# First attention batch: q and k loaded in rows of four tokens, queries turned and keys summed by TensorE

## The chip, the cores and the metric

One core of one Trainium2 chip runs the whole kernel. The metric is the device time of one execution in microseconds; before the change it is 1469.86 us, the median of three runs (1468.98 to 1470.56).

## What is computed

Attention over pooled keys and values, then two feed-forward blocks, all in float32:

```python
# q, k, v: (8 batches, 8 heads, 576 tokens, 64)
k_p = k.reshape(B, H, Sp, 8, D).mean(axis=3)      # keys and values are means over eight tokens
v_p = v.reshape(B, H, Sp, 8, D).mean(axis=3)
scores = scale * np.matmul(q, k_p.transpose(0, 1, 3, 2))
attn = softmax(scores)                            # 576 x 72 for each head
x = np.matmul(attn, v_p)                          # to (4608 tokens, 512)
x = ((x @ w1) * (x @ w2)) @ w3 @ w_out            # d_ff 1024
h = x @ w_in                                      # d_ff 2048
out = (h / (1 + np.exp(-1.702 * h))) @ w_out2
```

The weights are float64. They are loaded as pairs of 32-bit words and turned into float32 on the chip.

## The kernel before

The kernel has three stages. In the first, 40 weight tiles are loaded (`Conv.load`, L151, 512 KB each), converted (`Conv.step`: two passes of ScalarE, L166 and L168, a shift on VectorE, L169, an integer sum on GpSimd, L172) and split into a rounded part and a rest (`split`, L104 and L105). The sixteen tiles of `w3` among them are turned by TensorE (L508) and multiplied with `w_out` (`w3_mm`, by `mm3`, L114 to L116, into the banks `acc0` and `acc1`), so that the two matrices become one. `mm3` makes one product of near-float32 precision from three products of rounded parts, 128 x 512 each. In the second stage nine blocks of 512 tokens go through `w1`, `w2` and the combined matrix; in the third they go through the second feed-forward block (L709 and on). From about 118 us on, TensorE runs the products of the second and third stages almost without a gap.

The attention is cut into 32 groups: one batch and two heads each (`NG`). The steps of a group (`g0` to `g6`) are spread over calls of `tick`: one call for each step of the weight conversion in the first stage, two for each of the eight steps of a block in the second. The first batch's four groups (`NPE`, numbers 0 to 3) run in the first stage by `tick_first`, which overlaps two groups. They use two sets of banks in turn (`banks_of`): `wk[2:]` for even groups, `acc[2:]` for odd ones.

What the change touches is the beginning of a group. `g_load(n)` brings k and q (tiles `kr` and `qr`, 128 partitions x 576) by `load_blocks`: four DMAs for each, whose pieces are 32 numbers of one token (128 B), so that each 32 x 32 block stands where VectorE's block transpose turns it into place. `g0(n)` then makes, on VectorE, `kT` from `kr` (L255), `qT` from `qr` (L256), and the sums of eight tokens `ks` from `kT` (L258). ScalarE copies them to the two corners of `kbd` (L260, L261), so that one product serves both heads, and the load of the next group is issued. `g1(n)` multiplies `qT` with `kbd` on TensorE (L277, five products of 144 columns) into the group's two banks, and VectorE takes the maxima and differences. Later steps take the exponential (L293), normalise it (L300 to L303), turn it (`g4`: TensorE for the first four groups, L351 to L361), and multiply it with the pooled values (`g6`, L380 to L383).

All loads are issued by SP's queue, in one order. A scheduler arranges each engine's instructions when the kernel is built; each engine and each queue then works through its own list in order.

Of the kernel before, what the change touches and what calls it, by code (L numbers as in the profile page):

```python
# [7 lines left out]
F32 = mybir.dt.float32  # L8
# [4 lines left out]
ALU = mybir.AluOpType  # L13
# [4 lines left out]
P = 128  # L18
T = 512
# [3 lines left out]
def pooled_attention_moe_moe2(  # L23
# [18 lines left out]
    nc = tc.nc  # L42
    B, H, S, D = q.shape
    NT, DM = out.shape
    POOL = 8
    SK = S // POOL
# [9 lines left out]
    NPE = HP  # L56
# [28 lines left out]
    def take(shape=(P, 2, T), dtype=F32R):  # L85
        pool, i = free.pop(0)
        t = pool.tile(list(shape), dtype, name=f"s{i}", tag=f"s{i}")
        held[id(t)] = (t, pool, i)
        return t

    def take_a(i, dtype=F32R):

        return slota_p.tile([P, 2, T], dtype, name=f"s{i}", tag=f"s{i}")
# [30 lines left out]
    def sl(i, n=P):  # L124
        return slice(i * n, (i + 1) * n)
# [65 lines left out]
    with pa_ctx:  # L191
        pa = pa_ctx.enter_context(tc.tile_pool(name="pa", bufs=1))
# [6 lines left out]
            out=mask[:, 0], in_=mask[:, 0], compare_op=ALU.is_gt, fill=0.0,  # L199
            base=SK, pattern=[[0, D]], channel_multiplier=-1)  # L200
        nc.gpsimd.affine_select(
            out=mask[:, 1], in_=mask[:, 1], compare_op=ALU.is_ge, fill=0.0,
            base=-SK, pattern=[[0, D]], channel_multiplier=1)
        qT = pa.tile([P, TT * P], F32, name="qT")
        nc.vector.memset(qT[:, S:], 0.0)
        kbd = pa.tile([P, 2, SK], F32, name="kbd")
# [4 lines left out]
        for t in s_ts:  # L211
# [3 lines left out]
        ident = pa.tile([P, P], F32, name="ident")  # L215
        nc.gpsimd.memset(ident, 1.0)
        nc.gpsimd.affine_select(
            out=ident, in_=ident, compare_op=ALU.is_equal, fill=0.0,
            base=0, pattern=[[-1, P]], channel_multiplier=1)
        vm = pa.tile([P, 2, 2 * D], F32R, name="vm")  # L220
        vt = pa.tile([96, 2 * D], F32R, name="vt")
        nc.gpsimd.memset(f32(vt), 0.0)
# [2 lines left out]
        g_q, g_k, g_v, g_s = {}, {}, {}, {}  # L225

        def load_blocks(dst, src, b, hp):
            for c in range(4):
                nc.sync.dma_start(  # L229
                    dst[32 * c:32 * c + 32],  # L230
                    src[b, 2 * hp + c // 2, :, 32 * (c % 2):32 * (c % 2) + 32].rearrange(
                        "(g t) d -> t g d", t=32))

        def g_load(n):
            if n >= NG:
                return
            b, hp = divmod(n, HP)
            g_k[n] = pa.tile([P, S], F32, name="kr", tag="raw", bufs=4).rearrange("p (g d) -> p g d", d=32)
            load_blocks(g_k[n], k, b, hp)
            g_q[n] = pa.tile([P, S], F32, name="qr", tag="raw", bufs=4).rearrange("p (g d) -> p g d", d=32)  # L240
            load_blocks(g_q[n], q, b, hp)
# [9 lines left out]

        def g0(n):
            kr, qr = g_k.pop(n), g_q.pop(n)
            kT = pa.tile([P, S], F32, name="kT", tag="kT")
            nc.vector.transpose(out=kT, in_=kr.rearrange("p g d -> p (g d)"))  # L255
            nc.vector.transpose(out=qT[:, :S], in_=qr.rearrange("p g d -> p (g d)"))  # L256
            ks = pa.tile([P, SK], F32, name="ks", tag="ks")
            nc.vector.tensor_reduce(  # L258
                out=ks, in_=kT.rearrange("p (s u) -> p s u", u=POOL), op=ALU.add, axis=AX.X)
            nc.scalar.copy(kbd[:D, 0], ks[:D])  # L260
            nc.scalar.copy(kbd[D:, 1], ks[D:])  # L261
            g_load(n + 1)

        def banks_of(n):
            return acc[2:] if n < NPE and n % 2 else wk[2:]
# [132 lines left out]
        def x_slot(j, c):  # L398
            if (j, c) not in xs:
                xs[j, c] = take()  # L400
            return xs[j, c]
# [3 lines left out]
        def tick_first():  # L405

            t = tick_n[0]
            tick_n[0] += 1
            for n in range(NPE):
                if t == 2 * n + 6:  # L410
                    g6(n)
            for n in range(NPE):
                s = t - 2 * n
                if s == 0 and n == 0:
                    g0(0)
                elif s == 1:
                    g1(n)
                elif s == 2:
                    g2(n)
                    g0(n + 1)  # L420
                elif s == 3:
                    g3(n)
                elif s == 4:
                    g4(n)
                    g_va(n)
                elif s == 5:
                    g_vb(n)
            if t == 2 * NPE + 4:
                tick_n[0] = 4 * NPE
                give(s_sl)  # L430

        def tick():
            t = tick_n[0]
            if t < 4 * NPE:
                return tick_first()
            tick_n[0] += 1
            n, s = divmod(t, 4)
            if s == 0:
                if NPE <= n - 1 < NG:
                    g4(n - 1)  # L440
            elif s == 1:
                if n < NG:
                    g1(n)
            elif s == 2:
                if NPE <= n - 1 < NG:
                    g6(n - 1)
                if n < NG:
                    g2(n)
                    g_va(n)
                if n + 1 < NG:  # L450
                    g0(n + 1)
            elif n < NG:
                g3(n)
                g_vb(n)
# [92 lines left out]
        for jh in range(2):  # L547
            for i in range(4):
                j = jh * 4 + i
# [12 lines left out]

        conv.load()
        g_load(0)
        v_load(0)
        n3 = 8 + 2 * NIT
# [35 lines left out]
        for blk in range(NB):  # L602
            x = [x_slot(blk, c) for c in range(KM)]
            if blk == NB - 2:

                pa_ctx.close()
                pa = pa_ctx.enter_context(tc.tile_pool(name="pc", bufs=1, reuse_waits="tile"))
# [10 lines left out]
            for f in range(NF1):  # L618
# [6 lines left out]
                if blk == NB - 1:  # L625
                    give(w1_s.pop(f))
                    give(w2_s.pop(f))
                    if 0 <= f - FA < KM:

                        t = take_a(f - FA)  # L630
# [8 lines left out]
                u = u_s[blk, f] = take()  # L639
# [32 lines left out]
    with tc.tile_pool(name="pb", bufs=1, reuse_waits="tile") as pb, \  # L672
# [44 lines left out]
        def moving():  # L717
            i = mv_n[0] % NMV
            mv_n[0] += 1
            return pb.tile([P, 2, 2, T], F32R, name="mv", tag=f"mv{i}")  # L720
# [153 lines left out]
        x = x_first  # L874
# [9 lines left out]
        for k, f in enumerate(FO):  # L884
# [10 lines left out]
            g = moving()[:, :, 0]  # L895
# [20 lines left out]
        for pr in range(1, NPAIR + 1):  # L916
# [17 lines left out]
            for fp in range(NFP):  # L934
# [4 lines left out]
                for name, i in ORDER:  # L939
# [6 lines left out]
                    if name in PART:  # L946
                        s, h = PART[name]
# [13 lines left out]
                    elif name == "M2":  # L961
# [4 lines left out]
                        if i:  # L966
                            gelu(g11, g11)
                            g = mvs["M1", fp] = moving()
# [35 lines left out]
            src = {"M5": 0, "M7": 1, "M3": 2, "M2": 3, "M4": 3, "M6": 4}  # L1004
# [12 lines left out]
            m1, U, V, n = [], [], [], 0  # L1017
# [21 lines left out]
            for name, u in OUT:  # L1039
# [5 lines left out]
                if pr == NPAIR and name == "M3":  # L1045
# [7 lines left out]
                    for m in range(2):  # L1053
# [6 lines left out]
                        rows = out[b1 * T:(b1 + 1) * T]  # L1060
# [73 lines left out]
```

## Time and profile before

| | us |
|---|---|
| median of three runs | 1469.86 |
| the profiled execution's own time | 1471.6 |
| its span (first to last instruction) | 1469.5 |
| TensorE products busy | 1434.8 |
| VectorE, ScalarE, GpSimd busy | 985.2, 695.5, 489.3 |

The span is what the rows are taken from; the execution's own time holds 2.1 us around it. A busy share is an average over stages with different limits: here GpSimd works mainly in the first half, the DMA engines are full at the beginning and idle after it, and TensorE is busy nearly everywhere. The time between TensorE's busy time and the span, 34.7 us, is what all its waits come to.

### The profile page before, as it was taken

What the parts mean: (1) busy time and instruction counts of PE and PEld (TensorE: products, weight loads), DVE (VectorE), ACT (ScalarE), POOL (GpSimd) and SP (SyncE); (2) the same over time, 40 slices, a digit from 0 to 9 for tenths busy, and PEclk for the clock granted to TensorE, in tenths of its full rate; (3) what the DMA queues carried; (4) which work ended last, traced back from release to release, by engine and by line L of the source; (5) the groups of instructions that cost most, each with busy time, mean ns of one, the idle gap of its engine ahead of it and who ended that gap; (6) DMA issues with size and microseconds to landing.
All of it is one profiled execution on the core that took longest, in us unless ns stands there. A gap on an engine that the chain in (4) does not pass through costs nothing.

```text
span 1469.5 us, 19435 instructions
## 1 busy us (share of the span) xinstructions
PE 1434.8 (98%) x6536; PEld 1189.6 (81%) x6536; DVE 985.2 (67%) x1728; ACT 695.5 (47%) x1212; POOL 489.3 (33%) x589
## 2 busy tenths in 40 slices
PE   5979999999999999999999999999999999999998
PEld 4867888888888888888888888788888888888886
DVE  7878998878887887655636346783559354954554
ACT  7875344434333334366635334653455244534442
POOL 8789655554545555357743200000000000000000
PEclk9989999999999999999999999999999999999999
DMA  9993233323232311089869979867676766785665
GB/s 271 245 224 57 60 81 62 78 49 78 49 75 52 71 40 37 29 300 341 329 226 380 350 236 311 289 213 230 201 236 225 226 199 222 240 240 181 199 212 140
DMA packets 294435, 267.64 MB, mean 182 GB/s; under 512 B 201664, under 2 KB 226240, under 8 KB 294336
## 3 DMA queue, kind: packets, MB, share of 16 engines
q1 hardware_dynamic: 291648, 265.09, 60.0%
q10 hardware_dynamic: 2688, 1.31, 0.3%
q8 instruction: 52, 0.85, 0.2%
q14 instruction: 47, 0.39, 0.1%
HBM read 209.72 MB, written 56.62 MB: 181 GB/s over the span
## 4 chain that ended last, share of the span: by engine, by line
PE 89%; DMA 3%; DVE 2%; ACT 1%; SPq 1%; POOL 1%; issue 1%; DVEq 0%; ACTq 0%; POOLq 0%
PE bk L709 42%; PE wk L114 9%; PE wk L115 9%; PE wk L116 9%; PE acc L115 4%; PE acc L116 4%; PE acc L114 4%; PE wk L277 2%; DMA s<-in_moe_w_dram 1%; PE bk L116 1%; PE bk L114 1%; PE bk L115 1%; DMA wud<-wt 1%; SPq L229 1%; PE wk L381 1%
## 5 line engine op out<-in xcount | busy, mean ns | idle before, releaser
L709 PE MATMUL bk<-mv,st 128*128 128x512 f32 x1140 | 269.4, 389 | 0.0
L709 PE MATMUL bk<-xM,st 128*128 128x512 f32 x1104 | 262.1, 389 | 0.2 <-ACT u L972 0.2
L709 PEld LDWEIGHTS bk<-mv,st 128*128 128x128 f32 x1140 | 214.0, 188 | 44.4
L709 PEld LDWEIGHTS bk<-xM,st 128*128 128x128 f32 x1104 | 207.1, 188 | 44.0 <-ACT u L972 1.1
L114 PE MATMUL wk<-s,s 128*128 128x512 f32 x576 | 226.9, 396 | 1.9 <-ACT a L638 1.1
L116 PE MATMUL wk<-s,s 128*128 128x512 f32 x576 | 224.9, 391 | 1.3 <-DVE s L105 1.3
L115 PE MATMUL wk<-s,s 128*128 128x512 f32 x576 | 225.2, 392 | 1.0 <-DVE s L391 1.0
L314 DVE STREAM_TRANSPOSE p<-s_t 32x160 f32<-32x160 f32 (+1 forms) x560 | 178.5, 319 | 10.3
L114 PE MATMUL acc<-s,s 128*128 128x512 f32 x352 | 134.3, 404 | 9.3 <-DVE s L105 6.4
L115 PE MATMUL acc<-s,s 128*128 128x512 f32 x352 | 140.7, 400 | 1.2 <-POOL s L105 1.1
L116 PE MATMUL acc<-s,s 128*128 128x512 f32 x352 | 140.3, 398 | 0.0
L114 PEld LDWEIGHTS wk<-s,s 128*128 128x128 f32 x576 | 108.5, 189 | 24.6 <-ACT a L638 1.5
L116 PEld LDWEIGHTS wk<-s,s 128*128 128x128 f32 x576 | 108.5, 188 | 24.1 <-DVE s L105 1.5
L115 PEld LDWEIGHTS wk<-s,s 128*128 128x128 f32 x576 | 108.6, 189 | 23.4 <-DVE s L391 1.8
L105 DVE TENSOR_TENSOR mv<-g,mv 128x1024 fp32r<-128x1024 f32 x80 | 97.8, 1222 | 32.3 <-ACT mv L104 30.4
L104 ACT CAST mv<-g 128x1024 fp32r<-128x1024 f32 x80 | 84.3, 1054 | 72.0 <-PE bk L709 71.6
L172 POOL TENSOR_TENSOR cv<-cv,s 128x512 int32<-128x512 int32 x72 | 97.8, 1368 | 29.5 <-DVE cv L169 19.2
L105 POOL TENSOR_TENSOR s<-a,s 128x512 fp32r<-128x512 f32 x56 | 73.0, 1303 | 82.6 <-ACT s L104 62.7
L638 ACT COPY a<-wk 128x512 f32<-128x512 f32 x72 | 42.1, 585 | 112.1 <-PE wk L116 91.4
L114 PEld LDWEIGHTS acc<-s,s 128*128 128x128 f32 x352 | 67.8, 193 | 24.8 <-ACT s L104 5.0
L369 POOL TENSOR_TENSOR ph<-p,ph 128x576 fp32r<-128x576 f32 x32 | 45.6, 1424 | 125.3 <-ACT ph L368 122.7
L115 PEld LDWEIGHTS acc<-s,s 128*128 128x128 f32 x352 | 67.8, 192 | 15.2 <-POOL s L105 2.3
(190 smaller groups left out, 2355.7 us busy)
## 6 DMA issues: line engine op xcount, KB each, us to landing
st<-wud SPq DMA_DIRECT2D x95, 512.0 KB, 4.2
st<-wind SPq DMA_DIRECT2D x70, 512.0 KB, 4.7
st<-wind SPq DMA_DIRECT2D x70, 256.0 KB, 3.8
s<-in_moe_w_dram SPq DMA_DIRECT2D x32, 512.0 KB, 6.5
wind<-s SPq DMA_DIRECT2D x32, 512.0 KB, 5.5
s<-in_moe_w_out_dram SPq DMA_DIRECT2D x24, 512.0 KB, 6.7
kr<-in_k_dram SPq DMA_DIRECT2D x128, 72.0 KB, 2.6
qr<-in_q_dram SPq DMA_DIRECT2D x128, 72.0 KB, 2.6
```

The lines of the kernel that those rows point to most:

```text
L104: nc.scalar.copy(dst[:, 0], src)
L105: lo_eng.tensor_tensor(out=dst[:, 1], in0=src, in1=f32(dst[:, 0]), op=ALU.subtract)
L114: nc.tensor.matmul(o, a[:, 0, a_sl], b[:, 0, b_sl], start=first, stop=False)
L115: nc.tensor.matmul(o, a[:, 0, a_sl], b[:, 1, b_sl], start=False, stop=False)
L116: nc.tensor.matmul(o, a[:, 1, a_sl], b[:, 0, b_sl], start=False, stop=last)
L172: nc.gpsimd.tensor_tensor(out=w.bitcast(I32), in0=w.bitcast(I32), in1=lo_w.bitcast(I32), op=ALU.add)
L229: nc.sync.dma_start(dst[32 * c:32 * c + 32], src[b, 2 * hp + c // 2, :, 32 * (c % 2):32 * (c % 2) + 32].rearrange("(g t) d -> t g d", t=32))
L277: nc.tensor.matmul(sc[half][:, i * KW:(i + 1) * KW], qT[:, sl(tt)], mov, start=True, stop=True)
L314: nc.vector.transpose(out=dst[:, :nt, 32 * c:32 * c + 32], in_=s_t[32 * c:32 * c + 32, :nt, 32 * r:32 * r + 32])
L369: nc.gpsimd.tensor_tensor(out=ph[:, 1], in0=s0, in1=f32(ph[:, 0]), op=ALU.subtract)
L638: nc.scalar.copy(a, pa_)
L709: nc.tensor.matmul(o, w[:, x, m], b[:, y], start=first and n == 0, stop=last and n == 2, skip_group_check=True)
```

## The change

For the first four groups, k and q are loaded in rows of four tokens: partition p of a head's tile receives tokens 4p to 4p + 3 of the first 512 (1 KB in one piece), and the last 64 tokens follow with 256 B each (`load_rows`, eight DMAs for a group, as before). The tokens now stand on the partitions and the 64 numbers of a token in a row, so neither the block transposes nor the sum along a row fit, and TensorE takes their place. A constant tile `sums` holds ones where token row and pooled key belong together: four products for each head (L278, 64 x 64), one for each of the four tokens of a partition, add up the keys of the first 512 tokens in the second score bank, and one more (L288) adds those of the last 64. Products with the identity turn the queries (L283, four for each head, 64 x 128) into the first score bank and the last 64 tokens (L291) into the second. The two heads write the two halves of the partitions, by `tile_position`. ScalarE copies the sums to `kbd` and the turned queries to `qT`, putting the four tokens of a partition back in order with a step of four; VectorE copies the tail. The first four groups have no `kT`, no `ks` tile and no block transposes any more. Groups 4 to 31 are loaded and turned as before.

```diff
@@ -217,6 +217,13 @@
         nc.gpsimd.affine_select(
             out=ident, in_=ident, compare_op=ALU.is_equal, fill=0.0,
             base=0, pattern=[[-1, P]], channel_multiplier=1)
+        sums = pa.tile([P, D + 2 * POOL], F32, name="sums")
+        nc.gpsimd.memset(sums, 1.0)
+        for c0, cn, u in ((0, D, 2), (D, 2 * POOL, POOL)):
+            for base, sign in ((0, 1), (u - 1, -1)):
+                nc.gpsimd.affine_select(
+                    out=sums[:, c0:c0 + cn], in_=sums[:, c0:c0 + cn], compare_op=ALU.is_ge,
+                    fill=0.0, base=base, pattern=[[-sign * u, cn]], channel_multiplier=sign)
         vm = pa.tile([P, 2, 2 * D], F32R, name="vm")
         vt = pa.tile([96, 2 * D], F32R, name="vt")
         nc.gpsimd.memset(f32(vt), 0.0)
@@ -231,10 +238,22 @@
                     src[b, 2 * hp + c // 2, :, 32 * (c % 2):32 * (c % 2) + 32].rearrange(
                         "(g t) d -> t g d", t=32))
 
+        def load_rows(dst, src, b, hp):
+            for h in range(2):
+                rows = src[b, 2 * hp + h]
+                nc.sync.dma_start(
+                    dst[:, sl(h, 4 * D)], rows[:T].rearrange("(p j) d -> p (j d)", j=4))
+                nc.sync.dma_start(dst[sl(h, D), T:], rows[T:])
+
         def g_load(n):
             if n >= NG:
                 return
             b, hp = divmod(n, HP)
+            if n < NPE:
+                for g, x in ((g_k, k), (g_q, q)):
+                    g[n] = pa.tile([P, S], F32, name="raw", tag="raw", bufs=4)
+                    load_rows(g[n], x, b, hp)
+                return
             g_k[n] = pa.tile([P, S], F32, name="kr", tag="raw", bufs=4).rearrange("p (g d) -> p g d", d=32)
             load_blocks(g_k[n], k, b, hp)
             g_q[n] = pa.tile([P, S], F32, name="qr", tag="raw", bufs=4).rearrange("p (g d) -> p g d", d=32)
@@ -251,6 +270,35 @@
 
         def g0(n):
             kr, qr = g_k.pop(n), g_q.pop(n)
+            if n < NPE:
+                sc = banks_of(n)
+                tail, ks = sc[1][:, :S - T], sc[1][:, S - T:S - T + SK]
+                for j in range(4):
+                    for h in range(2):
+                        nc.tensor.matmul(
+                            ks[sl(h, D), :D], kr[:, sl(4 * h + j, D)], sums[:, :D],
+                            start=j == 0, stop=j == 3, tile_position=(0, h * D))
+                for j in range(4):
+                    for h in range(2):
+                        nc.tensor.matmul(
+                            sc[0][sl(h, D), sl(j)], qr[:, sl(4 * h + j, D)], ident,
+                            start=True, stop=True, tile_position=(0, h * D))
+                for h in range(2):
+                    hd = sl(h, D)
+                    nc.tensor.matmul(
+                        ks[hd, D:], kr[hd, T:], sums[hd, D + h * POOL:D + (h + 1) * POOL],
+                        start=True, stop=True, tile_position=(h * D, h * D))
+                    nc.tensor.matmul(
+                        tail[hd], qr[hd, T:], ident[hd, hd],
+                        start=True, stop=True, tile_position=(h * D, h * D))
+                nc.scalar.copy(kbd[:D, 0], ks[:D])
+                nc.scalar.copy(kbd[D:, 1], ks[D:])
+                nc.scalar.copy(
+                    qT[:, :T].rearrange("p (t j) -> p j t", j=4),
+                    sc[0].rearrange("p (j t) -> p j t", j=4))
+                nc.vector.tensor_copy(qT[:, T:S], tail)
+                g_load(n + 1)
+                return
             kT = pa.tile([P, S], F32, name="kT", tag="kT")
             nc.vector.transpose(out=kT, in_=kr.rearrange("p g d -> p (g d)"))
             nc.vector.transpose(out=qT[:, :S], in_=qr.rearrange("p g d -> p (g d)"))
```

On TensorE, group 0 stands before the change as follows: the five score products come straight after the `w3` products (`acc`), and L508 turns weight tiles. In these rows `s` are weight slots, `wk` and `acc` banks, and the sizes are those of the output.

```order
L508 MATMUL wk_70<-ident,cv 128x128 x4
L115 MATMUL acc_66<-s_303,s_202 128x512
L116 MATMUL acc_66<-s_303,s_202 128x512
L115 MATMUL acc_67<-s_303,s_246 128x512
L116 MATMUL acc_67<-s_303,s_246 128x512
L277 MATMUL wk_72<-kbd,qT 128x144 x3
L277 MATMUL wk_73<-kbd,qT 128x144 x2
L114 MATMUL acc_66<-s_339,s_409 128x512
```

In the same place of TensorE's list there now stand the twenty products of group 0; the score products (L325 now) follow two weight turns later (L556 is L508).

```order
L115 MATMUL acc_67<-s_292,s_269 128x512
L116 MATMUL acc_67<-s_292,s_269 128x512
L278 MATMUL wk_73<-sums,raw 64x64 x8
L283 MATMUL wk_72<-ident,raw 64x128 x8
L288 MATMUL wk_73<-sums,raw 64x8
L291 MATMUL wk_73<-ident,raw 64x64
L288 MATMUL wk_73<-sums,raw 64x8
L291 MATMUL wk_73<-ident,raw 64x64
L556 MATMUL wk_70<-ident,cv 128x128 x4
L114 MATMUL acc_66<-s_343,s_208 128x512
```

TensorE now has 80 more products in its list (20 for each of four groups), and everything behind them waits for them and for the loads that they read. For groups 1 to 3 they are mixed with `w3` products, so that the list changes 26 times between products of the whole array and products with a `tile_position` of one head, or between the two kinds of the latter.

On SP's queue, the first weights, k, q and v of group 0 and the next weight stand before the change as:

```order
L151 DMA s_154<-in_moe_w_out_dram 128x1024
L229 DMA kr<-in_k_dram 32x18x32 x4
L229 DMA qr<-in_q_dram 32x18x32 x4
L249 DMA vr<-in_v_dram 128x512
L250 DMA vtr<-in_v_dram 16x512
L151 DMA s_174<-in_moe_w_dram 128x1024
```

and now as (the two heads in turn, 512 tokens and then 64):

```order
L151 DMA s_160<-in_moe_w_out_dram 128x1024
L244 DMA raw<-in_k_dram 128x256
L246 DMA raw<-in_k_dram 64x64
L244 DMA raw<-in_k_dram 128x256
L246 DMA raw<-in_k_dram 64x64
L244 DMA raw<-in_q_dram 128x256
L246 DMA raw<-in_q_dram 64x64
L244 DMA raw<-in_q_dram 128x256
L246 DMA raw<-in_q_dram 64x64
L268 DMA vr<-in_v_dram 128x512
L269 DMA vtr<-in_v_dram 16x512
L151 DMA s_180<-in_moe_w_dram 128x1024
```

The number of issues is the same; the pieces of each are fewer and longer, and the tenth weight tile still stands behind all of them.

## Rows read from the trace of the kernel before

**Rows 1.** The page, first part: span; busy time, share and instructions of each engine.

```profile
span 1469.5 us, 19435 instructions
PE 1434.8 (98%) x6536; PEld 1189.6 (81%) x6536; DVE 985.2 (67%) x1728; ACT 695.5 (47%) x1212; POOL 489.3 (33%) x589
```

**Rows 2.** Windows of the first stage: engines' busy time, granted clock, DMA share, GB/s.

```profile
8.68:42.00 33.32, 26.51 (x103) 18.34 (x104) 29.18 (x40) 26.30 (x53) 30.21 (x29) 0.90 1.00 272
42.00:74.60 32.60, 32.60 (x180) 26.73 (x180) 26.47 (x45) 27.87 (x58) 22.95 (x24) 1.00 0.93 245
74.60:118.20 43.60, 32.46 (x134) 25.67 (x134) 35.80 (x59) 33.22 (x72) 37.95 (x45) 0.84 0.97 202
```

**Rows 3.** Waits of TensorE, 0 to 130 us: total, times, longest.

```profile
PE wk L508 <- POOL cv L172: 10.1, 2, 8.7
PE acc L114 <- DVE s L105: 6.4, 3, 3.4
```

**Rows 4.** TensorE's timeline: start, duration, instruction, idle time before it and its releaser.

```profile
76.84 0.53 PE L380 MATMUL acc<-ph,vm 128*128 128x288 f32 x1 [2.16 <-DVE s L284]
95.33 0.79 PE L114 MATMUL acc<-s,s 128*128 128x512 f32 x1 [3.36 <-DVE s L105]
```

**Rows 5.** The chain that ended last, in order of time: start, duration, what.

```profile
73.58 5.34 DMA qr<-in_q_dram
88.47 4.27 DMA kr<-in_k_dram
105.26 7.45 DMA s<-in_moe_w_dram
```

**Rows 6.** Windows with one kind of load: weights of 4 KB, q and k, weights of 1 KB.

```profile
50.00:55.00 5.00, 5.00 (x28) 4.22 (x27) 5.00 (x10) 4.07 (x8) 4.48 (x8) 1.00 0.99 370
85.00:89.00 4.00, 4.00 (x23) 3.34 (x21) 3.95 (x7) 3.32 (x9) 3.84 (x4) 1.00 0.99 131
106.00:110.00 4.00, 2.69 (x14) 2.11 (x13) 4.00 (x8) 2.74 (x8) 4.00 (x4) 1.00 1.04 335
```

**Rows 7.** SP's timeline: four DMAs of k (group 3); one of v, 128 pieces.

```profile
50.09 9.59 SPq L229 DMA_DIRECT2D kr<-in_k_dram  x4
43.18 0.44 SPq L249 DMA_DIRECT2D vr<-in_v_dram  x1
```

**Rows 8.** TensorE's timeline: products of 512 columns in a row, at either level of the clock.

```profile
98.48 0.63 PE L115 MATMUL acc<-s,s 128*128 128x512 f32 x1
98.90 0.63 PE L116 MATMUL acc<-s,s 128*128 128x512 f32 x1
101.43 0.39 PE L114 MATMUL acc<-s,s 128*128 128x512 f32 x1
101.65 0.40 PE L115 MATMUL acc<-s,s 128*128 128x512 f32 x1
```

**Rows 9.** TensorE's timeline: score products, turns, and two turns of fewer columns and rows.

```profile
70.00 1.39 PE L277 MATMUL acc<-kbd,qT 128*128 128x144 f32 x10
65.82 0.60 PE L508 MATMUL wk<-ident,cv 128*128 128x128 f32 x4
61.41 0.27 PE L360 MATMUL acc<-ident,s 128*32 128x128 f32 x1
61.61 0.23 PE L361 MATMUL acc<-ident,s 64*32 64x64 f32 x1
```

**Rows 10.** Groups by form, 0 to 122 us: count, busy us, mean ns, idle before.

```profile
L172 POOL TENSOR_TENSOR cv<-cv,s 128x512 int32<-128x512 int32 x36 | 48.2, 1343 | 12.2 <-ACT s L168 4.3 <-DVE cv L169 2.2 <-issue 1.2
L255 DVE STREAM_TRANSPOSE kT<-kr 128x576 f32<-128x576 f32 x8 | 6.2, 772 | 4.5 <-DMA kr<-in_k_dram 4.0 <-issue 0.4
L258 DVE TENSOR_REDUCE ks<-kT 128x72 f32<-128x576 f32 x7 | 5.2, 739 | 0.0
L352 ACT COPY p<-wk 128x512 f32<-128x512 f32 x2 | 1.2, 588 | 0.7 <-PE wk L351 0.7
```

**Rows 11.** GpSimd's timeline: its first weight, with the idle time before it.

```profile
5.63 1.29 POOL L172 TENSOR_TENSOR cv<-cv,s 128x512 int32<-128x512 int32 x1 [2.96 <-ACT s L168]
```

## The prediction

> **What bounds the kernel now.** I began with the page's first part: TensorE is busy for 1434.8 of 1469.5 us [rows 1], so all its waits together are 34.7 us, and a change can win only there or by making its work shorter. The windows then say where the waits lie. The first weight reaches TensorE after 8.7 us [rows 3]; between there and 42 us it is idle for 33.3 - 26.5 = 6.8 us, between 42 and 74.6 not at all, between 74.6 and 118.2 for 43.6 - 32.5 = 11.1 us [rows 2]. Only 8.1 us are left for the 1351 us behind. The change concerns the two stretches with 17.9 us of waits.
>
> What TensorE waits for there is a split weight or a step of the attention on VectorE: the largest waits are 2.16 us at 76.84 and 3.36 us at 95.33 [rows 4], and three waits for the rest of a split make 6.4 us [rows 3]. The chain of waits shows what stands behind them: VectorE's list is held up by a block transpose whose q landed 5.34 us after its issue at 73.58, then by a k that took 4.27 us from 88.47, and at the end by a weight that took 7.45 us from 105.26 [rows 5]. The DMA engines are full all through: shares of 1.00, 0.93 and 0.97 in the three windows [rows 2]. So **in this stage the DMA queue is the tightest resource**, with GpSimd and VectorE (38.0 and 35.8 of 43.6 us in the third window) behind it.
>
> The waits cost a second time. [...] After the wait of 95.33, products of 512 columns start 0.42 us apart, later 0.22 [rows 8]; there are twelve such, 12 x 0.20 = 2.4 us lost.
>
> **The change, part by part.**
>
> *Loads.* A group's k and q are 589,824 bytes in pieces of 128 B. While nothing else is loaded the full queue moves them at 131 GB/s, weights in pieces of 1 KB at 335 and of 4 KB at 370 [rows 6]. Four groups, 2.36 MB, take 18.0 us of all sixteen engines. In the new form eight ninths are pieces of 1 KB (2.10 MB at 335 GB/s: 6.3 us) and one ninth pieces of 256 B, for which no row stands; at the rate of 128 B they take 2.0 us, at that of 1 KB 0.8. I take the slower: 8.3 us, **9.7 us of full queue saved**, out of some 113. SP's queue gains too: four DMAs of k held it for 9.59 us, while one DMA of v with 128 pieces takes 0.44 [rows 7]. Eight DMAs a group then are about 3.5 us, and the weights behind them are issued earlier. The five further groups loaded before 118 us keep their small pieces.
>
> *VectorE, ScalarE, GpSimd.* VectorE loses two transposes of 0.77 and a sum of 0.74 us a group [rows 10], 2.3 us, and gains a copy of 64 columns, between 0.1 and 0.6 us by the 512-column copy of 0.59: some 8 us less in all. ScalarE gains one copy of 512 columns, 0.59 us [rows 10] if its step of four in the output costs nothing, up to twice that if it does: 2.4 to 4.7 us, on an engine that is busy for 33.2 of 43.6 us. GpSimd's five further constants come before its first weight, where it is idle for 2.96 us [rows 11]; they cost nothing as long as that cover is longer than about 1 us.
>
> *TensorE's new work.* Plain float32 products run as two instructions: the five score products are ten rows. With the 0.27 us of a single short row (L360) taken off for the last one, these ten start 0.12 us apart ((1.39 - 0.27) / 9), for 144 columns, and four turns of 128 columns 0.11 us apart ((0.60 - 0.27) / 3) [rows 9]. So a row needs about 0.11 us for 128 columns and, going by columns, 0.06 for 64. Per group: 16 rows of L283 at 0.11 make 1.8 us, 16 of L278 at 0.06 make 1.0, and the eight rows of L288 and L291 at 0.06 make 0.5, together 3.25 us; four groups, **13.0 us if one row follows the other**. The two heads of a pair write different halves of the columns of the array; if they run side by side it is half, 6.5. No row shows a product with a position, so I take the middle, 9.8.
>
> The list changes 26 times between kinds of product. A turn over 64 rows of the array (L361) starts 0.20 us after one over 128 (L360), which itself started 0.11 after its own neighbour [rows 9]: 0.09 us for a change, 2.3 us for 26. [...]
>
> So TensorE gets 12.1 us more (ends: 6.5 + 2.3 = 8.8 and 13.0 + 2.3 = 15.3). It stands in front of `w3` products and is paid in full unless it falls into a wait.
>
> *What it gets back.* With the queue relieved by a tenth and SP by tens of us, the waits of the third window should mostly go: of 11.1 us I take back 9, and of the time at the lower clock there (between 2.4 and 7.0 us) 3.5. The middle window shows that TensorE runs without a gap when weights are ahead [rows 2]. In the first window some 2 us belong to the start of the chain of conversions; of the rest I take 2.5 of waits and 1 of clock. Together **16 us**. The ends are 8 (five groups still come in small pieces, and GpSimd is busy for 84% of its time) and 22 (all of it). What is late next would be GpSimd's sum L172, 36 times 1.34 us [rows 10].
>
> **Sum:** 12 - 16 = -4.0 us. The profiled execution took 1471.6 us, 1.7 above the median of the runs; from the median it is 1469.9 - 4.0 = **1465.9 us**.
>
> **The rivals.**
>
> *Slower: TensorE pays more than it gets back.* TensorE works in order, so the new products stand in front of weights that are ready, and a late load now stops TensorE itself and not only VectorE. If no two rows run side by side (15.3 us) and the queue, still full with groups 4 to 8, keeps half of the waits (9 us back), the kernel takes 1476. It decides from the point at which less is won than added. For it: the middle window, where TensorE has no wait to fill and groups 1 to 3 add their products. Against it: the queue was full, and the chain runs through it three times. Chance 0.20.
>
> *Much faster: the heads run side by side and the waits go.* 8.8 added and 18 won back: 1460.7. For it: the products of the two heads alternate and use different columns. Against it: no row before shows two products at once. [...] Chance 0.25.
>
> *No difference: the saved transfers did not count.* If GpSimd and ScalarE keep the pace of the conversion, TensorE's new work just fills its waits: 12 added, 12 won, 1469.9. For it: GpSimd is busy for 38.0 of 43.6 us. Against it: its own waits, 12.2 us before L172 [rows 10], are partly the DMAs' too. Chance 0.20.
>
> **How the numbers follow.** The forecast has 0.35. Of it 0.28 lies beyond 0.2% (2.9 us, about what a measurement of this kernel can tell from no change) and 0.07 within. Faster is 0.28 + 0.25 + 0.03 of the third rival = 0.56; same 0.07 + 0.15 + 0.01 = 0.23; slower 0.19 + 0.02 = 0.21. The range runs from just below the second rival, 1459.5, to 1473, which leaves out the dear half of the first and the far ends of the sum.
>
> **What would show it.** Right: in the windows of the changed kernel DMA shares clearly below 0.97 in the third window, TensorE's busy time and idle time both changed, fewer than 5 us of waits between 74 us and the end of the stage, a granted clock above 0.9 there, and L283 rows 0.06 to 0.11 us apart. Wrong: waits of TensorE for k or q themselves, waits of the same size that now end with GpSimd or ScalarE, rows of the new products further apart than 0.12 us, or a ScalarE copy to `qT` of over a microsecond. The second and third stages should be as they were.

## The result, and the profile after

The changed kernel takes 1484.35 us (median of 4 runs, 1482.25 to 1484.67), the kernel before in the same runs 1470.21: a ratio of 1.0094 (95% interval [1.0082, 1.0107]), 14 us slower. The forecast was 1465.9, and the range ended at 1473.

The page's first part, the windows (the fourth holds the beginning of the second stage) and TensorE's waits up to 240 us of the changed kernel:

```profile
span 1483.0 us, 19755 instructions
PE 1444.6 (97%) x6696; PEld 1195.9 (81%) x6696; DVE 977.7 (66%) x1720; ACT 697.9 (47%) x1216; POOL 489.0 (33%) x594
```

```profile
8.68:42.00 33.32, 26.93 (x178) 20.09 (x179) 23.41 (x35) 27.79 (x55) 29.67 (x29) 0.95 0.88 307
42.00:74.60 32.60, 31.98 (x225) 25.27 (x223) 22.05 (x40) 26.80 (x56) 22.37 (x28) 1.00 0.80 238
74.60:118.20 43.60, 35.72 (x172) 28.55 (x171) 31.21 (x59) 33.75 (x75) 37.92 (x48) 0.92 0.75 179
118.20:240.00 121.80, 115.67 (x536) 95.74 (x535) 109.60 (x250) 54.73 (x121) 82.93 (x107) 0.97 0.28 59
```

```profile
PE wk L556 <- POOL cv L172: 12.0, 2, 9.0
PE acc L399 <- DVE s L351: 3.7, 1, 3.7
PE wk L114 <- ACT a L686: 3.5, 2, 2.0
PE wk L114 <- DVE a L689: 2.1, 1, 2.1
PE acc L114 <- ACT s L104: 1.9, 2, 1.2
```

Against [rows 1, 2], three things can be read. The queue was relieved as meant: shares of 0.88, 0.80 and 0.75 in place of 1.00, 0.93 and 0.97. TensorE's busy time grew by 9.8 us. But its idle time did not shrink: 1483.0 - 1444.6 = 38.4 us in place of 34.7. In the third window it fell, from 11.1 to 7.9 us; in the fourth, where nothing was changed, it is 121.80 - 115.67 = 6.1 us, where the kernel before has 0.8:

```profile
118.20:240.00 121.80, 121.03 (x584) 1.00 0.30 62
```

(A window with TensorE alone: length, busy time, granted clock, DMA share, GB/s.) That stretch is what the experiments had to explain.

### The profile page after: what moved, and what is told of

Same layout as the page of the kernel before. It is cut to its first block, busy times and chain, and to the rows that moved or that the text cites. A ratio compares the mean times of both kernels' runs of the same rounds, so it can differ in the third digit from the quotient of the medians.

```text
span 1483.0 us, 19755 instructions
## 1 busy us (share of the span) xinstructions
PE 1444.6 (97%) x6696; PEld 1195.9 (81%) x6696; DVE 977.7 (66%) x1720; ACT 697.9 (47%) x1216; POOL 489.0 (33%) x594
## 3 DMA queue, kind: packets, MB, share of 16 engines
q1 hardware_dynamic: 276288, 265.09, 58.6%
## 4 chain that ended last, share of the span: by engine, by line
PE 88%; DVE 5%; DMA 3%; POOL 1%; issue 1%; ACT 1%; SPq 0%; DVEq 0%; ACTq 0%; POOLq 0%
PE bk L757 42%; PE wk L114 8%; PE wk L115 8%; PE wk L116 8%; PE acc L116 5%; PE acc L115 5%; PE acc L114 5%; PE wk L325 2%; PE bk L114 1%; PE bk L115 1%; PE bk L116 1%; DVE cv L169 1%; DMA s<-in_moe_w_dram 1%; DVE p L362 1%; DMA wud<-wt 1%
```

## The experiments

Four theories stood at the beginning, and the expectations name them by letter. **A**: TensorE pays for its new products in full, and the queue's relief is worth nothing. **B**: the relief is worth what I forecast, and the products cost 20 us or more. **C**: the products only fill waits, and the loss comes from ScalarE's copy or from the issues on SP. **D**: any edit makes the scheduler set the lists anew, and that alone moves the time by 4 us or more.

### The parts one by one, and a control without new work

Four kernels, each built like any other. The loads alone:

```diff
             b, hp = divmod(n, HP)
+            if n < NPE:
+                for g, x in ((g_k, k), (g_q, q)):
+                    t = pa.tile([P, S], F32, name="raw", tag="raw", bufs=4)
+                    load_rows(t, x, b, hp)
+                    g[n] = t.rearrange("p (g d) -> p g d", d=32)
+                return
```

> The kernel before, in which only the loads of the first four groups are those of the change (rows of four tokens into the same tiles); everything else, VectorE's block transposes too, stays, so q and k of the first batch are scrambled. Theory A (the loads never held TensorE for long; the change lost by its products, which are paid in full, and the relief of the DMA queue buys next to nothing): within 2 us of the kernel before, and TensorE's idle time in the first 140 us stays near 26 us. Theory B (the relief buys what was forecast, and the products with what follows from them cost 20 us and more): 8 to 14 us faster than before, with TensorE idle for 17 us or less there.

The products alone: the kernel before with `sums` and the twenty products at the head of `g0` for the first four groups, `kr` and `qr` being read as they lie.

> The kernel before, with its loads, block transposes and sums, to which only the 80 products of the change and the constant tile are added; their results are not used (the score products overwrite them). Theory A (products paid in full): 8 to 12 us slower than before, TensorE's busy time about 9 us longer. Theory B (products and their knock-on cost over 20 us without the relief): 17 us slower or more. Theory C (the products fill waits, the loss comes from the copy to qT by ScalarE or from the loads' issue): less than 4 us slower.

The change with the queries put in order by TensorE's writes and not by ScalarE:

```diff
-                            sc[0][sl(h, D), sl(j)], qr[:, sl(4 * h + j, D)], ident,
+                            sc[0][sl(h, D)].rearrange("p (t j) -> p j t", j=4)[:, j], qr[:, sl(4 * h + j, D)], ident,
...
-                nc.scalar.copy(
-                    qT[:, :T].rearrange("p (t j) -> p j t", j=4),
-                    sc[0].rearrange("p (j t) -> p j t", j=4))
+                nc.scalar.copy(qT[:, :T], sc[0])
```

> The changed kernel, in which the turning products themselves write the queries with a step of four into the score bank, so that ScalarE's copy to qT has no step. The copy should fall from 1.07 to some 0.6 us. If ScalarE's copy is on the path (theory C): 2 to 4 us faster than the changed kernel, so at most 12 us slower than before. If not (theory A): within 1.5 us of the changed kernel, so 12 to 16 us slower than before.

And the control, in which the first four groups load q ahead of k and nothing else is different:

```diff
-            g_k[n] = pa.tile([P, S], F32, name="kr", tag="raw", bufs=4).rearrange("p (g d) -> p g d", d=32)
-            load_blocks(g_k[n], k, b, hp)
-            g_q[n] = pa.tile([P, S], F32, name="qr", tag="raw", bufs=4).rearrange("p (g d) -> p g d", d=32)
-            load_blocks(g_q[n], q, b, hp)
+            for g, x, name in ((g_q, q, "qr"), (g_k, k, "kr")) if n < NPE else ((g_k, k, "kr"), (g_q, q, "qr")):
+                g[n] = pa.tile([P, S], F32, name=name, tag="raw", bufs=4).rearrange("p (g d) -> p g d", d=32)
+                load_blocks(g[n], x, b, hp)
```

> A control: the kernel before with q loaded ahead of k in the first four groups, no work added or removed. If the order that the scheduler makes of an edited kernel matters little (theories A to C): within 2 us of before. If any edit of these loads can move the time by its reordering alone (theory D): 4 us or more to either side.

| | median, us | against before |
|---|---|---|
| loads alone | 1479.33 | 1.0053 [1.0034, 1.0072] |
| products alone | 1482.08 | 1.0083 [1.0062, 1.0103] |
| queries ordered by TensorE | 1483.61 | 1.0094 [1.0065, 1.0123] |
| control, q ahead of k | 1484.83 | 1.0091 [1.0076, 1.0106] |

The control costs as much as the change. Its windows and its longest waits:

```profile
8.68:42.00 33.32, 24.53 (x104) 17.16 (x105) 27.74 (x39) 26.17 (x54) 29.61 (x29) 0.95 0.96 265
42.00:74.60 32.60, 31.04 (x164) 24.64 (x162) 22.66 (x45) 24.69 (x51) 19.95 (x22) 1.00 0.87 226
74.60:118.20 43.60, 31.94 (x140) 25.16 (x140) 31.93 (x54) 34.17 (x76) 37.37 (x43) 0.86 0.96 213
118.20:240.00 121.80, 114.65 (x527) 94.55 (x527) 101.14 (x237) 51.70 (x117) 82.92 (x116) 0.95 0.29 61
```

```profile
PE wk L507 <- POOL cv L172: 9.9, 2, 8.8
PE acc L114 <- ACT s L104: 9.4, 5, 4.2
PE wk L115 <- DVE s L390: 4.7, 1, 4.7
```

It too has 7.2 us of idle time in the fourth window. What the four have in common is not work but the scheduler: after any edit it sets the lists of all engines anew. Of the 6,376 products in TensorE's list of the kernel before, 946 stand at another place in the control and 1,066 in the changed kernel, the last of them the 3,908th. The third kernel keeps the change's lists; its copy by ScalarE takes 0.58 us in place of 1.07, and its ratio is the same 1.0094, though the interval is too wide to exclude the 2 to 4 us of theory C. By the expectations the products alone, 11.3 us slower, fit A, and the loads alone, 8.6 us slower, neither A nor B; but the control, which has neither, fits D. None of the four tells what loads and products are worth by themselves.

### The same, with every engine's list held in the order before

So I read each engine's order from the built kernel before and gave it to the others: every instruction that they share is tied behind its predecessor of that order, on the same engine, without a semaphore. Where an instruction was replaced, the new one takes its place; a group's twenty products stand 6 (first group) or 12 `w3` products ahead of its scores. (The lines are written out here; in the kernels the lists stand packed.)

```diff
         pooled_attention_moe_moe2(tc, *args)
+        by = {i.name: i for i in nc.cur_bb.bb.instructions}
+        for names in ORDER:
+            for a, b in zip(names, names[1:]):
+                tc.add_manual_dep(
+                    by[b], a, mybir.DependencyInfo(
+                        mybir.DependencyClass.NoSync, mybir.DependencyReason.DATA),
+                    reason="order")
```

The control, the loads, the products and the change in that order:

> The control again (q loaded ahead of k in the first four groups, no work changed), but with every engine's instructions fixed in the order of the kernel before; only on SP the four loads of q and the four of k change places. If the 14 us of the control came from the other order that the scheduler made of the program (theory D), they go: 1470.8, at most 3 us off. If they came from the loads' places themselves (k, which is needed first, lands later), the time stays at 1480 to 1485 and DVE's first transposes of k still end the waits.

> The row loads alone in the first four groups (the queries and keys of batch 0 are scrambled by it), every engine in the order of the kernel before. If the queue's relief is worth what I forecast of it (9 to 16 us of waits), 1455 to 1462. If it is worth nothing because PE waits for conversions and not for weights (theory A), 1468 to 1473, with the DMA share lower and PE's idle time as before. If the 8.6 us that the loads cost in the run before were their own and not the order's, 1477 to 1481.

> The eighty products alone (results unused), every engine in the order of the kernel before; a group's twenty stand 6 (first group) or 12 step products ahead of its scores. If they are paid in full (A): about 2.3 us a group, 1479 to 1481, PE busy time +9 to +10 and its idle time as before. If they fall into waits (C): 1471 to 1475, idle time 5 us or more lower. If the order alone made the 11 us of the run before (D): under 1473 too, but with the idle time unchanged that cannot be.

> The change itself, with all that it shares with the kernel before in that kernel's order on every engine, and its products placed as in the run of the products alone. It is the sum of the two runs beside it if nothing new waits: A, nothing gained by the loads: 1479 to 1482. B, relief as forecast: 1464 to 1470. If D is the whole loss: 1470 or less. If a new wait (the turned queries' copy on ScalarE, 1.07 us, ahead of the scores) matters: 3 us or more above the sum, with scores that wait for ScalarE.

| in the order before | median, us | against before (1471.69) |
|---|---|---|
| control, q ahead of k | 1471.56 | 1.0002 [0.9993, 1.0011] |
| loads alone | 1464.94 | 0.9959 [0.9946, 0.9973] |
| products alone | 1471.01 | 0.9997 [0.9989, 1.0006] |
| the change | 1473.79 | 1.0017 [1.0008, 1.0026] |

The control is back at the time of the kernel before: the whole of its 14 us was the order. The loads are worth 6.8 us, between the ranges of B and A. The products cost nothing; as C has it, TensorE's idle time falls instead, to 1468.3 - 1439.6 = 28.7 us. And the change, which holds both, costs 2.1. That is 9 to 10 us more than the sum of its parts, and there were two candidates: a wait of the change's own, or one stock of waits used twice.

### Products earlier, and one engine's order at a time

In the change of the last table VectorE stood still for 7.4 us, because its copy of the last 64 queries had the place of the old sum, ahead of which the products had not yet run (VectorE's timeline, and the copy by ScalarE that it waited for):

```profile
66.88 0.23 DVE L439 TENSOR_TENSOR s<-wk,s 128x64 fp32r<-128x64 f32 x1 [0.38 <-ACT s L438]
74.47 0.23 DVE L299 COPY qT<-acc 128x64 f32<-128x64 f32 x1 [7.36 <-ACT kbd L295]
73.99 0.21 ACT L294 COPY kbd<-acc 64x72 f32<-64x72 f32 x1 [3.94 <-PE acc L291]
```

The first of the next four kernels moves the products to 20, 22 and 32 `w3` products ahead and that copy later. The other three are the change with one part of the lists held as in this one and the rest left to the scheduler (`ORDER` then has the lists of those engines only).

> The change in the order of the kernel before, as in the run of that name, with its products earlier on TensorE (20, 22 and 32 step products ahead of the scores of the second, third and fourth group, not 12) and the 64-column copy on VectorE later (1.0 to 1.2 us ahead of the scores' time in the kernel before), so that it waits for no product. If the 9 us by which the change in that order missed the sum of its two parts (-6.8 and -0.7) were VectorE's and ScalarE's waits for the late products (7.4 us in one place), most of them come back: 1464 to 1468. If they are the queue's relief and the products taking the same waits twice (both fill the idle time of 74.6 to 118.2), it stays at 1472 to 1475.

> The change with TensorE alone fixed in the order of the run beside it, the scheduler free to set the other engines. If what the scheduler's order costs (1484.4 for the change against 1473.8 in the order before) lies in the order of TensorE's products: 1465 to 1475. If it lies in the loads' order or in that of the conversions: 1480 or more.

> The change with SP's issues alone in the order of the kernel before (the weights' loads then come as early among q, k and v as there), the other engines as the scheduler sets them. If the loads of w1 and w2 that the changed order puts behind those of v are the loss: 1470 to 1476. If the order of TensorE or of the conversions is: 1480 or more.

> The change with VectorE, ScalarE and GpSimd in the order of the kernel before and TensorE and SP as the scheduler sets them (it keeps TensorE close to the order before: 440 places differ, not 1,066). If the order of the copies and conversions decides: 1465 to 1475. If the loads' or the products' does: 1480 or more.

| the change, lists held | median, us | against before (1471.31) |
|---|---|---|
| all, products earlier | 1471.05 | 1.0004 [0.9996, 1.0013] |
| TensorE's alone | 1480.56 | 1.0065 [1.0052, 1.0078] |
| SP's alone | 1479.68 | 1.0070 [1.0044, 1.0095] |
| VectorE's, ScalarE's and GpSimd's | 1472.01 | 0.9998 [0.9987, 1.0009] |

So the places of the products and of that copy were worth some 2 us: 2.1 above the kernel before of the same runs, then 0.3 below it. That lies between the two ranges, and VectorE still waits 2.6, 3.0, 1.2 and 2.3 us for its four copies. TensorE's or SP's order alone brings back some 4 of the 14 us (with SP's, single runs go from 1476.9 to 1487.7). That of VectorE, ScalarE and GpSimd brings back all: the order that matters is that of the copies and conversions, and with those three lists held, what the scheduler itself makes of TensorE and SP does as well as the old order. (It then also leaves TensorE's list closer to the old one; but that list held to the letter did not do it.) TensorE's windows of that kernel:

```profile
8.68:42.00 33.32, 29.93 (x171) 0.90 0.90 312
42.00:74.60 32.60, 31.66 (x234) 1.00 0.87 257
74.60:118.20 43.60, 39.35 (x183) 0.92 0.70 163
118.20:240.00 121.80, 119.10 (x575) 1.00 0.30 62
```

Its idle time in the four windows is 3.4 + 0.9 + 4.3 + 2.7 = 11.3 us; the changed kernel has 6.4 + 0.6 + 7.9 + 6.1 = 21.0. These 9.7 us are most of the 12.3 between the two medians. Which of the moved conversions is the dear one, I did not try.

### One stock of waits, or a wait of the change's own

> Row loads and the eighty products together, but the products' results unused and VectorE's transposes and sums kept (the queries and keys of batch 0 are scrambled), every engine in the order of the kernel before, the products 6, 20, 22 and 32 step products ahead of the scores. If loads and products take up the same waits: 1469 to 1473, as the change in that order (1471.1). If the change's own copies eat the gain: 1463 to 1466, the sum of the two parts (-6.8 and -0.7).

> The change for the first group alone (its 20 products, 8 row loads; the three other groups as before), every engine in the order of the kernel before. Its products fall where TensorE waits anyway (after the first group all versions were 1 us or less behind at 33 us), and a quarter of the loads' 6.8 us is 1.7: 1468.5 to 1470.5 if the relief goes by the byte. If relief is in the later loads alone (those of 45 to 75 us): 1471 to 1472.5.

> Keys alone in rows and summed by TensorE (10 products a group, about 1 us), queries loaded in blocks and turned by VectorE as before, every engine in the order of the kernel before. Half the relief (-3.4) against 40 products, of which three groups, 3 us, lie where TensorE has no idle time: 1469.5 to 1472 if relief and products share the waits; 1466 to 1469 if the products fall into waits, as they did alone. Slower than 1473 if the sums, now from TensorE, are late for ScalarE.

The first is the two parts put together, with nothing of the change's copies. In the second `n < NPE` in `g_load` and `g0` becomes `n < 1`. The third, in `g0`:

```diff
             if n < NPE:
-                sc = banks_of(n)
-                tail, ks = sc[1][:, :S - T], sc[1][:, S - T:S - T + SK]
+                ks = banks_of(n)[1][:, S - T:S - T + SK]
...
-                nc.scalar.copy(
-                    qT[:, :T].rearrange("p (t j) -> p j t", j=4),
-                    sc[0].rearrange("p (j t) -> p j t", j=4))
-                nc.vector.tensor_copy(qT[:, T:S], tail)
+                nc.vector.transpose(out=qT[:, :S], in_=qr.rearrange("p g d -> p (g d)"))
```

| in the order before | median, us | against before (1470.73) |
|---|---|---|
| loads and products, no new copies | 1469.78 | 0.9993 [0.9984, 1.0002] |
| the change for the first group alone | 1469.64 | 0.9990 [0.9981, 1.0000] |
| keys alone in rows | 1468.68 | 0.9989 [0.9980, 0.9997] |

Without the new copies the two parts still come to -1.0 us and not to -7.4: they share the waits. The first group alone (-1.1) and keys alone (-2.1, in the range set for products that fall into waits) do not decide it: their intervals overlap that of the two parts. Since the order is the same, one instruction can be followed through all traces. The score products' line, 60 to 126 us, in the kernel before, the loads alone, the products alone, the change with earlier products and the two parts together (duration, then first and last start; `acc` is group 3, `wk` groups 4 and 5):

```profile
L277 PE MATMUL acc<-kbd,qT x10: 286/286/288, 70.0 to 71.1; 128*128 128x144 f32 x10
L277 PE MATMUL wk<-kbd,qT x20: 283/285/286, 102.6 to 122.3; 128*128 128x144 f32 x20
```

```profile
L290 PE MATMUL acc<-kbd,qT x10: 286/286/288, 70.2 to 71.3; 128*128 128x144 f32 x10
L290 PE MATMUL wk<-kbd,qT x20: 283/286/448, 93.6 to 114.8; 128*128 128x144 f32 x20
```

```profile
L306 PE MATMUL acc<-kbd,qT x10: 286/286/288, 75.8 to 76.9; 128*128 128x144 f32 x10
L306 PE MATMUL wk<-kbd,qT x20: 283/286/448, 98.3 to 120.7; 128*128 128x144 f32 x20
```

```profile
L325 PE MATMUL acc<-kbd,qT x10: 286/286/288, 75.3 to 76.4; 128*128 128x144 f32 x10
L325 PE MATMUL wk<-kbd,qT x20: 283/286/448, 98.1 to 119.3; 128*128 128x144 f32 x20
```

```profile
L319 PE MATMUL acc<-kbd,qT x10: 286/286/288, 75.5 to 76.6; 128*128 128x144 f32 x10
L319 PE MATMUL wk<-kbd,qT x20: 283/286/442, 98.3 to 118.4; 128*128 128x144 f32 x20
```

At group 3's scores the loads have won nothing (+0.2 us), and every kernel with the products is 5.3 to 5.8 us late: the middle window has no gap to hide them in. From there to the last scores the loads alone win 122.3 - 114.8 + 0.2 = 7.7 us, the products alone 1.6 + 5.8 = 7.4, the change 3.0 + 5.3 = 8.3, both parts 3.9 + 5.5 = 9.4. Whichever comes, relieved loads or a TensorE that arrives later, the 11.1 us of waits behind it give back 7 to 9 us, once. TensorE's third window says the same: 11.1 us of idle time before, 6.0 with the loads, 6.3 with the products, 5.5 with both (in this order):

```profile
74.60:118.20 43.60, 37.59 (x172) 0.92 0.76 157
74.60:118.20 43.60, 37.28 (x175) 0.92 0.88 212
74.60:118.20 43.60, 38.12 (x186) 0.96 0.72 166
```

How far single traces carry is shown by the control in the order before, whose profiled execution was 2.0 us faster than its median:

```profile
L276 PE MATMUL acc<-kbd,qT x10: 286/286/288, 71.1 to 72.2; 128*128 128x144 f32 x10
L276 PE MATMUL wk<-kbd,qT x20: 283/285/286, 100.8 to 119.8; 128*128 128x144 f32 x20
74.60:118.20 43.60, 33.99 (x152) 0.92 0.95 201
```

With nothing relieved and nothing added it wins 2.5 + 1.1 = 3.6 us in that stretch, and is idle for 9.6 in the window. So that the parts share one stock rests first on the medians (-6.8, -0.7, and -1.0 for both); the traces say where it lies.

## Why the prediction was wrong

*The queue: right.* The queue's packets took 60.0% of 1469.5 us before and 58.6% of 1483.0 after, 881.7 and 869.0 us: 12.7 saved, and 7.2 with the loads alone in the order before (59.8% of 1462.3). I had 9.7. (The front part calls the DMA engines idle behind the beginning. Their share is 0.30 in the fourth window and 0.75 from 600 us on, but TensorE is busy for 99% of the time there.)

*SP: wrong, and no run prices it.* I expected eight row loads in 3.5 us and SP relieved by tens of us. The eight issues of group 0 last 0.33 to 0.56 us, but they start 1.27 to 1.80 us apart, in SP's timeline (group 0: k and q in the kernel before; then the changed kernel's first k, last q, and the weight behind them):

```profile
5.76 7.27 SPq L229 DMA_DIRECT2D kr<-in_k_dram  x4
13.08 4.14 SPq L229 DMA_DIRECT2D qr<-in_q_dram  x4
```

```profile
5.87 0.33 SPq L244 DMA_DIRECT2D raw<-in_k_dram  x1
...
14.32 0.34 SPq L244 DMA_DIRECT2D raw<-in_q_dram  x1
15.65 0.47 SPq L246 DMA_DIRECT2D raw<-in_q_dram  x1
...
17.26 0.42 SPq L151 DMA_DIRECT2D s<-in_moe_w_dram  x1
```

The profile gives the time between them to earlier transfers of weights (8.3 us for L246 in the first 60): each of the eight starts 0.02 us after the landing of the load eight issues ahead, the first three at 5.87, 7.15 and 8.95 us behind weights that landed at 5.85, 7.13 and 8.93. So the length of an issue, which I reckoned with, does not set the pace here. These eight take 10.3 us, in place of 11.5; over the four groups, from each issue to the next, it is 38.1 us in place of 44.9.

*TensorE's new work: right in mechanism, inside the range.* TensorE's timeline, group 0:

```profile
18.52 0.39 PE L116 MATMUL acc<-s,s 128*128 128x512 f32 x1
18.83 0.69 PE L278 MATMUL wk<-sums,raw 128*64 128x64 f32 x16
19.35 1.04 PE L283 MATMUL wk<-ident,raw 128*64 128x128 f32 x16
20.32 0.29 PE L288 MATMUL wk<-sums,raw 64*64 64x8 f32 x4
20.46 0.32 PE L291 MATMUL wk<-ident,raw 64*64 64x64 f32 x4
20.72 0.66 PE L556 MATMUL wk<-ident,cv 128*128 128x128 f32 x4
```

Sixteen rows of L278 take 0.52 us and of L283 0.97, 0.03 and 0.06 us a row: half of the 0.11 of a single turn [rows 9] and of my 0.06 for 64 columns. The heads do run side by side. A product of 512 columns starts 0.22 us after its predecessor [rows 8], so the change of kind at 18.83 costs 0.31 - 0.22 = 0.09, as I took. The group needs 1.98 us from 18.74 on. But only group 0 stands in one piece here. Group 1 stands in two, and by the starts of the `w3` products around them (32.21 to 32.78 and 33.60 to 36.63, less 0.22 each) it needs 3.2. TensorE's busy time as a whole grew by 9.8 us, against my 12.1 and its lower end of 8.8.

*VectorE and ScalarE: inside my bounds.* ScalarE's copy to `qT` takes 1.06 to 1.09 us (0.59 to 1.2 expected), VectorE's of 64 columns 0.22.

*What it gets back: this step failed.* I took 16 us back, with ends of 8 and 22. The loads alone, in an unchanged order, are worth 6.8. More than that, I added the products in full on one side and took the waits back in full on the other, though the third rival, "no difference", already said that the products fill waits. The two draw on one stock, which gives back 7 to 9 us in all. In the order before, with its products earlier, the change has paid 5.3 us by group 3's scores, is 3.0 us ahead at 119.3, and keeps 0.3 of that to the end. The same score products of a later group start last at 247.6 us in the kernel before and at 246.0 in this one, so half of the lead is gone by then; what takes it I did not follow. The third rival was right about the work, and in the order before about the time too (1471.05 against 1471.31). Of the 16, 3.5 and 1 us stood for time at the lower clock, the first of them between 2.4 and 7.0; no run shows the 7.0, the 3.5 or the 1. What the traces show is a granted clock of 0.50 from 95.40 to 100.60 us in the kernel before, where products of 512 columns start 0.42 to 0.43 us apart, and of 1.00 from 101.00 to 102.50, where they start 0.22 to 0.24 apart; in the third window seventeen of them start at the longer distance in the kernel before and eight in the changed one, by my estimate 9 x 0.20 = 1.8 us less.

*What was missing: the order.* In the front part stands that a scheduler sets the lists; the sum put the new order at nothing, and no rival took it up. Of the signs that I had named, the DMA share, the clock of 0.92 and the rows of L283 came as for a right forecast; but the third window kept 7.9 us of waits and not fewer than 5, ScalarE's copy took over a microsecond, and the second stage did not stay as it was. The rival on the slower side priced TensorE's work (1476), and the kernel is slower by 14 us although that work is cheaper than I thought. Of the 14, between 10.6 (1484.35 - 1473.79) and 13.3 (1484.35 - 1471.05) go away when the lists are held, by where the products are put.

## What to carry to other kernels

Where a scheduler orders the program, an edit is two changes, the edit and a new order; run a control that alters nothing but the order of two independent loads, and hold the order before you credit or blame the edit. Work put ahead of a wait and a relief of what is waited for are not two gains (here -1.0 us together, not -7.4): follow one instruction through the traces and see where each is won. In the order before, keys alone in rows (1468.68, 0.9989) is the fastest version that leaves nothing out, 2 us below the kernel before; that is about what can be measured, and it does not stand clear of the change for the first group alone (1469.64).

## What the runs showed of the hardware

ScalarE's copy of 128 x 512 to `qT` took 1066 ns with a step of four numbers in its output and 578 without (groups by form, 0 to 60 us, the change and then the kernel with the queries ordered by TensorE):

```profile
L296 ACT COPY qT<-wk 128x512 f32<-128x512 f32 x2 | 2.1, 1066 | 0.0
L296 ACT COPY qT<-wk 128x512 f32<-128x512 f32 x2 | 1.2, 578 | 0.8 <-PE wk L283 0.8
```

The same step in TensorE's writes to a bank costs nothing here: sixteen rows of L283 take 0.97 us to the start of L288 in the second kernel (TensorE's timeline), as they do in the change (19.35 to 20.32, above):

```profile
20.95 1.05 PE L283 MATMUL wk<-ident,raw 128*64 128x128 f32 x16
21.92 0.29 PE L288 MATMUL wk<-sums,raw 64*64 64x8 f32 x4
```
